# A seven-product cross network: layer 0 multiplies by C + 1, and its product 3 is split into seven smaller products

## The chip, the cores and the metric

The kernel runs on one core of a Trainium2 chip. The metric is the device time of one execution in microseconds (us). A time is the median of several executions; the profile is of one further execution.

## The reference

A deep cross network of six layers. The batch has 16384 rows of 1024 features, in bf16.

```python
B, F, D, L = 16384, 100, 16, 6
Din = min(F * D, 1024)          # 1024
# x0 [B, Din], ws [L, Din, Din], bs [L, Din], all bf16
def reference(x0, ws, bs):
    x = x0
    L = ws.shape[0]
    for l in range(L):
        proj = jnp.einsum('bd,de->be', x, ws[l]) + bs[l]
        x = x0 * proj + x
    return x
```

In layer 0 the state x is x0 itself, so that layer's result is x0 * (proj + 1).

## The kernel before

**Tiling.** The batch is cut into 16 pairs of 1024 rows. Eight super-rounds s = 0..7 each take two pairs, A and B, through the six layers, and each layer of one pair is a *step*: A layer 0, B layer 0, A layer 1 and so on, 96 steps in all. The state is kept transposed, features on the partitions: a `big` tile is [128, 2, 8, 512], where the second axis n says which 512 rows of the pair, the third which block of 128 features. A pair has one such tile for x0 (`x0T`) and one for its state (`xst`). The state tiles of A and of B are the same two buffers (big2, big3) in every super-round; those of x0 alternate.

**Seven products.** A step multiplies a 1024 x 1024 weight matrix with 1024 x 1024 data by one level of the Winograd form of Strassen's method: seven products of 512 x 512 instead of eight. A product is 16 matmuls of 128 x 128 weights and 512 data columns (`mm`, line 403), four for each 128 output features m. Product 1 goes to the four PSUM banks `pA`; products 6, 7 and 4 are added there one after the other. Product 5 goes to the four banks `pX`, and product 3 is added to it. ScalarE (ACT) copies each stage out of PSUM, with the bias where a stage begins a result (lines 52 and 55): P1s (product 1), P5s (product 5), S53 (5 + 3), U2s (1 + 6), C2[:, 1] (1 + 6 + 7), C2[:, 0] (1 + 6 + 7 + 4).

Product 2 (in every step but the first) and product 4 (after super-round 0) are split once more, each into seven products of 256 x 256. `inner` (line 411) is one such half-size product: four matmuls with 256 data columns. "Wide" and "narrow" matmuls below are those with 512 and 256 columns. The half-size products need combined weights (ids 8 for product 2 and 9 for product 4) and combined data (`ti2`, `ti4`, four parts of 512 columns each, made by `inner_t` as two differences t02, then t1, then t3). Their results are collected in EA and EB (product 2), and E4 and e5 (product 4).

**VectorE (DVE)** does all other arithmetic as two-operand operations recorded by `vtt` (line 46), in program order. For a step X, with Y the step before it (`prev`), it runs: T13 (the data of products 5 and 7, 4096 columns); then, of Y, m1 (C12 times x0), s11 (C22: C2[:, 1] + P5s), a1 (plus the state); X's T2 (product 6's data); Y's s4 (the parts of E4 that need e5); X's T4 (product 4's data); Y's e4 (C2[:, 0] + E4); the ti4 differences; Y's mC2 and aC2 (both halves of C2 times x0, plus the state, 4096 columns each), with t1 and t3 of ti4 before and behind aC2. Later come EA + EB, P1s + EA, the ti2 of the next step with m0 and a0 (C11 times x0, plus the state) between, and U2s + S53. T13, T2, T4, ti2 and ti4 have one buffer each.

```python
for f in (m1, s11, a1, t2, s4, t4, e4, i02, mC2, i1, aC2, i3):
```

**PSUM.** Eight banks in two pools of four, which change roles each step. In the pool `psX` stand first the three banks of product 2's half-size products, then the four of pX, then z5 and z1 of product 4's; each new bank waits for the copies out of the one that had the buffer.

**Order of the second half of a step.** Product 3 follows product 5 (its first column before product 5's last), then for product 6 one column and one half-size product of product 4 in turn, then product 7, then the rest of product 4; its last half-size product is deferred behind the next step's first column.

**Transfers.** SyncE (SP) issues all DMAs, in order. Weights sit in a ring of nine tiles shared by A and B; loads for the next layer are issued in B steps (`prefetch_upto`, line 99) and wait for PE to free a ring tile. In super-round 0 VectorE makes the combined weights (`combo`) and SP stores them to `Lc` in DRAM (line 139), from where later super-rounds load them. When a pair has ended, `turn_pair` (line 321) transposes its state tile by DMA into its old x0 tile, in the following step, once aC2 has written the last part; `write_pair` (line 328) then stores it. So A's state tile of super-round s - 1 is read by the transpose issued in B's layer 5, and B's by the one issued in A's layer 0 of super-round s.

`evt("P2s")` is a [128, 4, 512] buffer that holds product 2 in the first step alone.

Of the kernel before, what the change touches and what calls it, by code (L numbers as in the profile page):

```python
# [17 lines left out]
def kernel(  # L18
# [7 lines left out]
    nc = tc.nc  # L26
# [49 lines left out]
    def bank(p):  # L76
        return p.tile([P, NB], FP32, name="px")

    Lc = dram.tile([L, 6, P, KH * H], BF16, name="Lc")
    CIDX = {5: 0, 6: 1, 7: 2, 3: 3, 8: 4, 9: 5}  # L80
    lc = lambda l, pid: Lc[l, CIDX[pid]].rearrange("p (k e) -> p k e", k=KH)

    def raw_src(l, pid):
# [38 lines left out]
    def combo(l, pid):  # L122
        if pid <= 7:
            a, op, b = {5: (lambda: raw12[l], ADD, lambda: W[0, l, 4]), 6: (lambda: W[0, l, 5], SUB, lambda: W[0, l, 1]),
                        3: (lambda: W[0, l, 2], SUB, lambda: W[0, l, 6]), 7: (lambda: W[0, l, 1], SUB, lambda: raw12[l])}[pid]
            if pid == 5:
                W[0, l, 5] = ei_pool.tile([P, KH, H], BF16, name=("eb", "e4")[l % 2])
            t = W[0, l, pid]
            vtt(t[:], a()[:], b()[:], op)
        else:  # L130
            w = W[0, l, {8: 2, 9: 4}[pid]]
            t = W[0, l, 8] if pid == 8 else ti_pool.tile([P, KH, H], BF16, name="ti4")
            i11, i12, i21, i22 = w[:, 0:2, 0:HE], w[:, 0:2, HE:H], w[:, 2:4, 0:HE], w[:, 2:4, HE:H]
            iv = t[:].rearrange("p k (j e) -> p k j e", e=HE)
            vtt(iv[:, 0], i12, i22, ADD)
            vtt(iv[:, 3], i11, i12, SUB)
            vtt(iv[:, 1], iv[:, 0], i11, SUB)
            vtt(iv[:, 2], i21, iv[:, 1], SUB)
        pin(nc.sync.dma_start(lc(l, pid), t[:]))
# [1 line left out]
    def sub4(t):  # L141
        return {(i, j): t[:, 2 * i:2 * i + 2, j * NQ:(j + 1) * NQ] for i in range(2) for j in range(2)}

    def inner_t(hold, src, name):

        def t02():
            ti = ti_pool.tile([P, 4, 2, NQ], BF16, name=name)
            setattr(hold, name, ti)
            b = sub4(src())
            vtt(ti[:, 0], b[0, 1], b[0, 0], SUB)  # L150
            vtt(ti[:, 2], b[1, 1], b[0, 1], SUB)

        def t1():
            ti = getattr(hold, name)
            vtt(ti[:, 1], sub4(src())[1, 1], ti[:, 0], SUB)

        def t3():
            ti = getattr(hold, name)
            vtt(ti[:, 3], sub4(src())[1, 0], ti[:, 1], SUB)

        return [t02, t1, t3]
# [42 lines left out]
    ones = const.tile([P, P], BF16, name="ones")  # L204
    signs = const.tile([P, P], BF16, name="signs")
    nc.vector.memset(ones[:], 0.0)
    nc.vector.memset(ones[0:1, :], 1.0)
    nc.vector.memset(signs[:], 0.0)
    nc.vector.memset(signs[0:2, :], 1.0)
    nc.vector.memset(signs[0:1, :], -1.0)  # L210
# [38 lines left out]
    vcopy(b_all[:], pb[:, 0:LK])  # L249

    cur = {"A": Pair(0, x0T_A), "B": Pair(1, x0T_B)}
    new = {}
# [8 lines left out]
    def trail(Y, store):  # L261

        if Y is None:
            return [None] * 7
        C2, E4, e5 = Y.C2, Y.E4, Y.e5
        eh1 = lambda t: t[:, :, KH:KD, :]
        m1, a1 = fin_of(Y, Y.C12, 0, 1)

        def s4():
            for i in range(2):  # L270
                vtt(E4[:, 2 * i:2 * i + 2, NQ:NB], E4[:, 2 * i:2 * i + 2, (1 - i) * NQ:(2 - i) * NQ], e5[:], ADD)

        def a1s():
            a1()
            if store:
                store_half(Y, 0)

        return [m1, lambda: vtt(C2[:, 1], C2[:, 1], Y.P5s[:], ADD), a1s,
                s4 if E4 is not None else None,
                (lambda: vtt(C2[:, 0], C2[:, 0], E4[:], ADD)) if E4 is not None else None,  # L280
                lambda: vtt(C2[:], C2[:], eh1(Y.x0T), MULT),
                lambda: vtt(eh1(Y.xst), C2[:], eh1(Y.src_in), ADD)]

    def fin_of(Y, C, eh, n):
        xs = half(eh)
        return [lambda: vtt(C, C, Y.x0T[:, n, xs, :], MULT),
                lambda: vtt(Y.xst[:, n, xs, :], C, Y.src_in[:, n, xs, :], ADD)]

# [42 lines left out]
    for s in range(NPAIR // 2):  # L331
        for l in range(L):
            for side in ("A", "B"):
                X, Y = cur[side], prev
                first, last = step == 0, (X.pr, l) == LAST
                in2, in4 = not first, s > 0 and not (s + 1 == NPAIR // 2 and l + 1 == L)
                psA, psX = ps[step % 2], ps[1 - step % 2]
                step += 1
                bias = lambda eh, m, l=l: b_all[:, l * KD + eh * KH + m: l * KD + eh * KH + m + 1]
# [5 lines left out]
                def bring(who, s=s, home=home):  # L345
                    pr = 2 * (s + 1) + (who == "B")
                    new[who] = Pair(pr, bigt(home["n" + who]))
                    load_x0(pr, new[who].x0T)

                if side == "A" and s + 1 < NPAIR // 2:  # L350
                    if l == (2 if s > 0 else L - 1):
                        pending.append(lambda: bring("A"))
                    if l == 3 and s > 0:
                        pending.append(lambda: bring("B"))

                if s + 1 == NPAIR // 2 and side == "A" and l == 2:
# [8 lines left out]
                    pending.append(load_rows)  # L365

                def end_of(Y, late):
                    if s + 1 == NPAIR // 2 and side == "A" and l == L - 1 and not late:
# [19 lines left out]
                def mm(pid, wt, pts, m, start):  # L388
                    rhs = X.rhs(pid)
                    if last:  # L390
                        pt = pts[m][:]
                        if pid == 1:
                            nc.tensor.matmul(pt, lhsT=ones[:], rhs=zero[:], start=True, stop=False)  # L393
                        elif pid == 7:
                            nc.tensor.matmul(pt, lhsT=signs[:], rhs=zero[:], start=False, stop=False, skip_group_check=True)  # L395
# [42 lines left out]
                ev(P1s, pA, 0, 0)  # L438
                t2, t4 = (None, None) if first else (X.T2, X.T4)
                i02, i1, i3 = inner_t(X, lambda: X.T[4], "ti4") if in4 else [None] * 3  # L440
                for f in (m1, s11, a1, t2, s4, t4, e4, i02, mC2, i1, aC2, i3):
                    if f is not None:
                        f()
                if in2:
# [36 lines left out]
                    mm(5, w5, pX, 1, True)  # L481
                    inner(cols(q1), wi[:, 3], ti[:, 2], False)
                    evi(ea[1, 1], q1)
                    mm(5, w5, pX, 2, True)
                    inner(cols(q1), wr[1, 1], ti[:, 3], False)
                    evi(ea[1, 0], q1)
                    ev(P5s, pX, 1)
                    ev(P5s, pX, 2)
                    end_of(Y, False)
                    w3 = weights(3)  # L490
                    mm(3, w3, pX, 0, False)
                    mm(5, w5, pX, 3, True)
                    ev(P5s, pX, 3)
                    ev(S53, pX, 0, 0)
                    if not last:
                        ev(P1s, pA, 3, 0)
                    for m in range(1, KH):
                        mm(3, w3, pX, m, False)
                        ev(S53, pX, m, 0)
# [59 lines left out]
                if s == 0:  # L559
# [9 lines left out]
                    elif l + 1 < L:  # L569
                        for pid in (5, 6, 3) if l == 0 else ():  # L570
                            combo(1, pid)
                        combo(l + 1, 7)
                        combo(l + 1, 8)
                w6 = weights(6)
                end_of(Y, True)
                if last:
# [4 lines left out]
                X.C2, X.P5s, X.l = C2, P5s, l  # L581
                if in4:
                    w4, w4i, w7 = weights(4), weights(9), weights(7)
                    wj, wr4 = w4i[:].rearrange("p k (j e) -> p k j e", e=HE), sub_w(w4, HE)
# [3 lines left out]
                    e4 = sub4(E4)  # L588
                    z5, z1 = bank(psX), bank(psX)
                    mm(6, w6, pA, 0, False)  # L590
                    ev(U2s, pA, 0)
                    inner(cols(z1), wr4[0, 0], b4[0, 0], True)
# [4 lines left out]
                    evi(X.e5[:], z5)  # L597
                    mm(6, w6, pA, 2, False)
                    ev(U2s, pA, 2)
                    inner(cols(z1), wj[:, 1], t4[:, 1], False)  # L600
                    evi(e4[0, 1], z1)
                    mm(6, w6, pA, 3, False)
                    ev(U2s, pA, 3)
                    mm(7, w7, pA, 0, False)
                    ev(C2[:, 1], pA, 0, 1)
                    inner(cols(z1), wj[:, 3], t4[:, 2], False)
                    evi(e4[1, 0], z1)
                    for m in range(1, KH):
                        mm(7, w7, pA, m, False)
                        ev(C2[:, 1], pA, m, 1)  # L610
                    col = lambda m0, j, pA=pA: (lambda m: pA[m0 + m][:, j * NQ:(j + 1) * NQ])
                    inner(col(0, 0), wr4[1, 0], b4[1, 0], False)
                    inner(col(0, 1), wj[:, 2], b4[1, 1], False)
# [79 lines left out]
```

## Time and profile before

| | |
|---|---|
| median of 3 runs | 2267.81 us (2267.52 to 2268.53) |
| the profiled execution, its own time | 2268.03 us |
| its span | 2266.2 us, 33559 instructions |
| busy share of the span | PE 100%, weight loads 56%, DVE 95%, ACT 84% |
| DMA | 334.59 MB, mean 148 GB/s |

Each line of a timeline has the start in us from the span's start, the busy time, the engine, the line of the kernel, the operation with output and inputs, the count of merged instructions, and in brackets the idle time before and what ended it. PE is TensorE's matmul, PEld its weight load, SPq the DMA queue of SP. Matmuls overlap, so their rate is read from starts.

### The profile page before, as it was taken

The page shows a single profiled execution, that of the slowest core. Times are in us where ns is not written, and L with a number is a line of the kernel's source. Part 1 is how long each engine was busy: PE and PEld are TensorE (multiplying, and loading weights), DVE is VectorE, ACT ScalarE, POOL GpSimd, SP SyncE. Part 2 cuts the span into 40 slices and gives each one's busy share as a digit, 9 for nine tenths or more (in the row PEclk, how much of TensorE's full clock was granted, in tenths as well). Part 3 has the DMA queues.
Part 4 walks back from the last instruction along what each step waited for, and adds up shares of the span by engine and source line. Part 5 has one row for each costly group of instructions (what it writes and reads, how often), then busy time and mean ns, then how long its engine had stood idle before and what let it go on. Part 6 is the DMA issues. An engine that isn't in the chain of part 4 may idle for free.

```text
span 2266.2 us, 33559 instructions
## 1 busy us (share of the span) xinstructions
PE 2259.2 (100%) x12925; PEld 1264.4 (56%) x12925; DVE 2161.6 (95%) x2394; ACT 1910.9 (84%) x3307; POOL 0.7 (0%) x6
## 2 busy tenths in 40 slices
PE   9999999999999999999999999999999999999999
PEld 4555555555555555555555555555555555555554
DVE  8999989999999999999999999999999999999999
ACT  6777788888888888888888888888888888888887
POOL 0000000000000000000000000000000000000000
PEclk9999999999999999999999999999999999999999
DMA  7423494523945239442494434944348443483337
GB/s 231 151 94 121 149 216 159 146 85 119 255 133 136 93 124 257 132 121 97 128 259 122 121 112 127 245 121 121 125 124 236 121 131 121 126 228 121 104 119 178
DMA packets 508452, 334.59 MB, mean 148 GB/s; under 512 B 390530, under 2 KB 470404, under 8 KB 508292
## 3 DMA queue, kind: packets, MB, share of 16 engines
q1 hardware_dynamic: 508292, 332.45, 51.7%
q8 instruction: 101, 1.65, 0.3%
q14 instruction: 59, 0.48, 0.1%
HBM read 213.92 MB, written 52.43 MB: 118 GB/s over the span
## 4 chain that ended last, share of the span: by engine, by line
PE 99%; DMA 0%; DVE 0%; SPq 0%; issue 0%; ACT 0%; DVEq 0%
PE px L403 74%; PE px L411 24%; PE px L398 1%; DMA wp<-in_ws_dram 0%; DVE cb L46 0%; SPq L120 0%; DVE eb L46 0%; DVE T L46 0%; DVE wp L46 0%; SPq L217 0%; PE px L395 0%; PE px L393 0%; ACT cb L52 0%; SPq L220 0%; DVEq L46 0%
## 5 line engine op out<-in xcount | busy, mean ns | idle before, releaser
L403 PEld LDWEIGHTS <-wp 128*128 128x128 bf16 x7344 | 718.5, 98 | 669.9 <-issue 0.8
L403 PE MATMUL px<-T,wp 128*128 128x512 bf16 x4384 | 1069.4, 379 | 0.0
L403 PE MATMUL px<-big,wp 128*128 128x512 bf16 x2960 | 712.4, 379 | 0.4 <-ACT big L52 0.4
L411 PEld LDWEIGHTS <-wp 128*128 128x128 bf16 x4752 | 465.0, 98 | 254.3
L55 ACT ACTIVATE cb<-px,b_all 128x512 bf16<-128x512 f32 x760 | 502.0, 686 | 85.3 <-PE px L403 71.4
L411 PE MATMUL px<-ti,wp 128*128 128x256 bf16 x2684 | 402.7, 273 | 0.0
L52 ACT CAST ea<-px 128x512 bf16<-128x512 f32 x344 | 201.6, 586 | 140.5 <-PE px L411 140.5
L46 DVE TENSOR_TENSOR T<-big 128x4096 bf16<-128x4096 bf16 (+1 forms) x97 | 220.1, 2269 | 71.0 <-PE px L403 71.0
L52 ACT CAST U2s<-px 128x512 bf16<-128x512 f32 x384 | 225.0, 586 | 64.4 <-PE px L403 61.4
L55 ACT ACTIVATE P1s<-px,b_all 128x512 bf16<-128x512 f32 x380 | 254.3, 695 | 6.0 <-PE px L403 4.4
L55 ACT ACTIVATE S<-px,b_all 128x512 bf16<-128x512 f32 x380 | 242.3, 703 | 0.8 <-PE px L403 0.8
L46 DVE TENSOR_TENSOR T<-big,T 128x2048 bf16<-128x2048 bf16 x192 | 234.1, 1219 | 1.4
L52 ACT CAST P5s<-px 128x512 bf16<-128x512 f32 x384 | 217.9, 596 | 17.7 <-PE px L403 17.5
L46 DVE TENSOR_TENSOR cb<-cb,big 128x4096 bf16<-128x4096 bf16 (+2 forms) x105 | 221.6, 2113 | 0.7 <-ACT cb L52 0.5
L46 DVE TENSOR_TENSOR big<-cb,big 128x4096 bf16<-128x4096 bf16 x95 | 217.2, 2286 | 0.5
L52 ACT CAST e<-px 128x512 bf16<-128x512 f32 x328 | 192.7, 588 | 0.0
L411 PE MATMUL px<-big,wp 128*128 128x256 bf16 x1084 | 162.6, 273 | 0.0
L52 ACT CAST eb<-px 128x512 bf16<-128x512 f32 x258 | 152.1, 590 | 6.2
L411 PE MATMUL px<-T,wp 128*128 128x256 bf16 x984 | 134.2, 273 | 0.0
L46 DVE TENSOR_TENSOR P1s<-P1s,big 128x2048 bf16<-128x2048 bf16 x106 | 129.3, 1220 | 3.3 <-ACT P1s L55 2.4
L46 DVE TENSOR_TENSOR S<-U2s,S 128x2048 bf16<-128x2048 bf16 (+1 forms) x97 | 117.2, 1208 | 2.5 <-ACT U2s L52 2.4
L46 DVE TENSOR_TENSOR S<-S,big 128x2048 bf16<-128x2048 bf16 (+1 forms) x99 | 118.5, 1197 | 0.1
(77 smaller groups left out, 1360.8 us busy)
## 6 DMA issues: line engine op xcount, KB each, us to landing
wp<-Lc SPq DMA_DIRECT2D x252, 512.0 KB, 4.6
wp<-in_ws_dram SPq DMA_DIRECT2D x144, 512.0 KB, 3.4
out_dram<-big SPq DMA_DIRECT2D x28, 1024.0 KB, 10.7
Lc<-big SPq DMA_DIRECT2D x15, 512.0 KB, 2.7
Lc<-wp SPq DMA_DIRECT2D x9, 512.0 KB, 2.7
ea<-in_ws_dram SPq DMA_DIRECT2D x6, 512.0 KB, 5.2
Lc<-ti SPq DMA_DIRECT2D x6, 512.0 KB, 3.1
big<-in_x_dram SPq DMA_DIRECT2D x1, 2048.0 KB, 9.9
```

Source lines behind the costliest of these rows:

```text
L46: return pin(nc.vector.tensor_tensor(out=out, in0=in0, in1=in1, op=op))
L52: return pin(nc.scalar.copy(out=out, in_=in_))
L55: return pin(nc.scalar.activation(out=out, in_=in_, func=IDENT, bias=bias, scale=1.0))
L398: nc.tensor.matmul(pt, lhsT=rhs[:, k, m * P:(m + 1) * P], rhs=wt[:, k, :], start=(start and k == 0 and pid != 1), stop=(k == KH - 1), **kw)
L403: nc.tensor.matmul(pts[m][:], lhsT=wt[:, k, m * P:(m + 1) * P], rhs=rhs[:, k, :], start=(start and k == 0), stop=(k == KH - 1), **kw)
L411: nc.tensor.matmul(dst(m), lhsT=w[:, k, m * P:(m + 1) * P], rhs=rhs[:, k, :], start=(start and m == 0 and k == 0), stop=(k == 1), skip_gro ...
```

## The change

In layer 0 the state added at the end is x0 itself. The change adds 1 to the biases of layer 0 when they are set up, multiplies by x0 straight into the state tile, and leaves out a1, a0 and aC2 there (the name aC2 is then that of nothing; mC2 writes the state). This holds in all 16 steps of layer 0.

In the 14 steps of layer 0 after super-round 0 (`in3`), product 3 is done by seven half-size products. Its combined weights have id 10; they are made in super-round 0 and loaded once per super-round into the buffer of P2s. Its combined data `ti3` (made by k02, k1, k3) lies in the second half of the pair's new state tile; the collected E3 lies in another quarter of it; e6 is a new small buffer. Three of the seven half-size products are added in pX, four go to two further banks y1 and y5. In the next step m1 completes E3 with e6, adds it to C12, and multiplies. The order of VectorE's work with ti3 differs between A and B. The two constant tiles `ones` and `signs` of the last step are set later, by GpSimd, in the ti4 buffer.

```diff
+    Lc = dram.tile([L, 7, P, KH * H], BF16, name="Lc")
...
+    pin(nc.vector.tensor_scalar_add(out=b_all[:, 0:KD], in0=pb[:, 0:KD], scalar1=1.0))
+    vcopy(b_all[:, KD:LK], pb[:, KD:LK])
...
+        if Y.E3 is not None:
+            def m1(E3=Y.E3, e6=Y.e6, C=Y.C12, mul=m1):
+                for i in range(2):
+                    vtt(E3[:, 2 * i:2 * i + 2, NQ:NB], E3[:, 2 * i:2 * i + 2, (1 - i) * NQ:(2 - i) * NQ], e6[:], ADD)
+                vtt(C, C, E3, ADD)
+                mul()
...
-                lambda: vtt(C2[:], C2[:], eh1(Y.x0T), MULT),
-                lambda: vtt(eh1(Y.xst), C2[:], eh1(Y.src_in), ADD)]
+                lambda: vtt(eh1(Y.xst) if Y.l == 0 else C2[:], C2[:], eh1(Y.x0T), MULT),
+                None if Y.l == 0 else (lambda: vtt(eh1(Y.xst), C2[:], eh1(Y.src_in), ADD))]
...
+        if Y.l == 0:
+            return [lambda: vtt(Y.xst[:, n, xs, :], C, Y.x0T[:, n, xs, :], MULT), None]
...
+                X.l, in3 = l, l == 0 and s > 0
...
+                if side == "B" and s + 1 < NPAIR // 2 and l == L - 1:
+                    w3i = evt("P2s")
+                    pending.insert(0, lambda w=w3i: pin(nc.sync.dma_start(w[:], lc(0, 10))))
...
-                for f in (m1, s11, a1, t2, s4, t4, e4, i02, mC2, i1, aC2, i3):
+                if in3:
+                    ti3 = X.xst[:, 0, KH:KD, :].rearrange("p q (k b) -> p q k b", k=2)
+                    k02, k1, k3 = inner_t(X, lambda: X.rhs(3), "ti3", ti3)
+                order = (m1, s11, a1, t2, k02, s4, k1, t4, k3, e4, i02, mC2, i1, aC2, i3)
+                if in3 and side == "B":
+                    order = (m1, s11, a1, t2, s4, t4, e4, k02, i02, k1, k3, mC2, i1, aC2, i3)
+                for f in order:
...
+                    if in3:
+                        ev(P5s, pX, 1)
                     mm(5, w5, pX, 2, True)
                     inner(cols(q1), wr[1, 1], ti[:, 3], False)
                     evi(ea[1, 0], q1)
...
+                        inner(colx(0, 0), wr3[1, 0], b3[1, 0], False)
+                        inner(colx(0, 1), wk[:, 2], b3[1, 1], False)
+                        ev(S53, pX, 0, 0)
+                        mm(5, w5, pX, 3, True)
+                        ev(P5s, pX, 3)
+                        ev(S53, pX, 1, 0)
+                        ev(P1s, pA, 3, 0)
...
                     mm(6, w6, pA, 0, False)
+                    if in3:
+                        inner(colx(2, 0), wr3[1, 1], t3[:, 3], False)
+                        ev(S53, pX, 2, 0)
+                        ev(S53, pX, 3, 0)
                     ev(U2s, pA, 0)
+                    if in3:
+                        y1, y5 = bank(psX), bank(psX)
+                        X.E3 = X.xst[:, 1, 0:KH, :]
...
+                    if in3:
+                        inner(cols(y1), wr3[0, 0], b3[0, 0], True)
+                        evi(e3[0, 0], y1)
...
```

The lines left out place the other three half-size products of y1 and y5 with their copies behind columns of products 6 and 7, make and store the combined weights, and set the two constant tiles.

More of the change, by code (lines that the diff above doesn't have):

```diff
@@ L77, in bank @@
         return p.tile([P, NB], FP32, name="px")
-    Lc = dram.tile([L, 6, P, KH * H], BF16, name="Lc")
-    CIDX = {5: 0, 6: 1, 7: 2, 3: 3, 8: 4, 9: 5}
+    Lc = dram.tile([L, 7, P, KH * H], BF16, name="Lc")
+    CIDX = {5: 0, 6: 1, 7: 2, 3: 3, 8: 4, 9: 5, 10: 6}
     lc = lambda l, pid: Lc[l, CIDX[pid]].rearrange("p (k e) -> p k e", k=KH)
@@ L130, in combo @@
         else:
-            w = W[0, l, {8: 2, 9: 4}[pid]]
+            w = W[0, l, {8: 2, 9: 4, 10: 3}[pid]]
             t = W[0, l, 8] if pid == 8 else ti_pool.tile([P, KH, H], BF16, name="ti4")
@@ L142, in sub4, with inner_t @@
         return {(i, j): t[:, 2 * i:2 * i + 2, j * NQ:(j + 1) * NQ] for i in range(2) for j in range(2)}
-    def inner_t(hold, src, name):
+    def inner_t(hold, src, name, tile=None):
         def t02():
-            ti = ti_pool.tile([P, 4, 2, NQ], BF16, name=name)
+            ti = tile if tile is not None else ti_pool.tile([P, 4, 2, NQ], BF16, name=name)
             setattr(hold, name, ti)
@@ L203 @@
     b_all = const.tile([P, LK], FP32, name="b_all")
[L204 to L210, printed above, removed]
     home = dict(xA=0, xB=1, sA=2, sB=3, nA=4, nB=5)
@@ L273, in a1s @@
         def a1s():
-            a1()
+            if a1 is not None:
+                a1()
             if store:
@@ L365 @@
                     pending.append(load_rows)
+                if s + 1 == NPAIR // 2 and side == "A" and l == L - 1:
+                    rowsel = ti_pool.tile([P, 4, 2, NQ], BF16, name="ti4")
+                    ones, signs = rowsel[:, 0, 0, 0:P], rowsel[:, 1, 0, 0:P]
+                    nc.gpsimd.memset(rowsel[:, 0:2, 0, 0:P], 0.0)
+                    nc.gpsimd.memset(ones[0:1, :], 1.0)
+                    nc.gpsimd.memset(signs[0:2, :], 1.0)
+                    nc.gpsimd.memset(signs[0:1, :], -1.0)
                 def end_of(Y, late):
@@ L392, in mm @@
                         if pid == 1:
-                            nc.tensor.matmul(pt, lhsT=ones[:], rhs=zero[:], start=True, stop=False)
+                            nc.tensor.matmul(pt, lhsT=ones, rhs=zero[:], start=True, stop=False)
                         elif pid == 7:
-                            nc.tensor.matmul(pt, lhsT=signs[:], rhs=zero[:], start=False, stop=False, skip_group_check=True)
+                            nc.tensor.matmul(pt, lhsT=signs, rhs=zero[:], start=False, stop=False, skip_group_check=True)
                         for k in range(KH):
@@ L440 @@
                 i02, i1, i3 = inner_t(X, lambda: X.T[4], "ti4") if in4 else [None] * 3
-                for f in (m1, s11, a1, t2, s4, t4, e4, i02, mC2, i1, aC2, i3):
+                X.E3 = None
+                k02, k1, k3 = [None] * 3
+                if in3:
[5 more added lines that the diff above has]
+                for f in order:
                     if f is not None:
@@ L486 @@
                     evi(ea[1, 0], q1)
-                    ev(P5s, pX, 1)
+                    if not in3:
+                        ev(P5s, pX, 1)
                     ev(P5s, pX, 2)
@@ L490 @@
                     w3 = weights(3)
[L491 to L495, printed above, removed]
-                        ev(P1s, pA, 3, 0)
-                    for m in range(1, KH):
-                        mm(3, w3, pX, m, False)
-                        ev(S53, pX, m, 0)
+                    if in3:
+                        wk, wr3 = w3i[:].rearrange("p k (j e) -> p k j e", e=HE), sub_w(w3, HE)
+                        b3, t3 = sub4(X.rhs(3)), X.ti3
+                        colx = lambda m0, j, pX=pX: (lambda m: pX[m0 + m][:, j * NQ:(j + 1) * NQ])
+                        inner(colx(0, 0), wr3[1, 0], b3[1, 0], False)
[4 more added lines that the diff above has]
+                        ev(S53, pX, 1, 0)
+                        ev(P1s, pA, 3, 0)
+                    else:
+                        mm(3, w3, pX, 0, False)
+                        mm(5, w5, pX, 3, True)
+                        ev(P5s, pX, 3)
+                        ev(S53, pX, 0, 0)
+                        if not last:
+                            ev(P1s, pA, 3, 0)
+                        for m in range(1, KH):
+                            mm(3, w3, pX, m, False)
+                            ev(S53, pX, m, 0)
                     vtt(e0(EA), e0(EA), e0(EB), ADD)
@@ L573 @@
                         combo(l + 1, 8)
+                        if l == 0:
+                            combo(0, 10)
                 w6 = weights(6)
@@ L580 @@
                 C2 = cb_pool.tile([P, 2, KH, NB], BF16, name="cb")
-                X.C2, X.P5s, X.l = C2, P5s, l
+                X.C2, X.P5s = C2, P5s
                 if in4:
@@ L590 @@
                     mm(6, w6, pA, 0, False)
+                    if in3:
+                        inner(colx(2, 0), wr3[1, 1], t3[:, 3], False)
+                        ev(S53, pX, 2, 0)
+                        ev(S53, pX, 3, 0)
                     ev(U2s, pA, 0)
+                    if in3:
+                        y1, y5 = bank(psX), bank(psX)
+                        X.E3 = X.xst[:, 1, 0:KH, :]
+                        X.e6 = ei_pool.tile([P, 2, NQ], BF16, name="e6")
+                        e3 = sub4(X.E3)
                     inner(cols(z1), wr4[0, 0], b4[0, 0], True)
@@ L597 @@
                     evi(X.e5[:], z5)
+                    if in3:
+                        inner(cols(y1), wr3[0, 0], b3[0, 0], True)
+                        evi(e3[0, 0], y1)
                     mm(6, w6, pA, 2, False)
@@ L601 @@
                     evi(e4[0, 1], z1)
+                    if in3:
+                        inner(cols(y5), wk[:, 0], t3[:, 0], True)
+                        evi(X.e6[:], y5)
                     mm(6, w6, pA, 3, False)
                     ev(U2s, pA, 3)
+                    if in3:
+                        inner(cols(y1), wk[:, 1], t3[:, 1], False)
+                        evi(e3[0, 1], y1)
                     mm(7, w7, pA, 0, False)
@@ L610 @@
                         ev(C2[:, 1], pA, m, 1)
+                        if in3 and m == 1:
+                            inner(cols(y1), wk[:, 3], t3[:, 2], False)
+                            evi(e3[1, 0], y1)
                     col = lambda m0, j, pA=pA: (lambda m: pA[m0 + m][:, j * NQ:(j + 1) * NQ])
```

1 line of the change is left out of this document (removed).

## The prediction

> **What bounds the kernel now.** I read the page first: busy times, the chain that ended last, the group that shows where VectorE (DVE) waits.
>
> ```profile
> PE 2259.2 (100%) x12925; PEld 1264.4 (56%) x12925; DVE 2161.6 (95%) x2394; ACT 1910.9 (84%) x3307; POOL 0.7 (0%) x6
> ...
> PE 99%; DMA 0%; DVE 0%; SPq 0%; issue 0%; ACT 0%; DVEq 0%
> ...
> L46 DVE TENSOR_TENSOR T<-big 128x4096 bf16<-128x4096 bf16 (+1 forms) x97 | 220.1, 2269 | 71.0 <-PE px L403 71.0
> ```
>
> TensorE (PE) is the chain; DVE idles 71 us, always for PE. A busy PE could still stall inside the modelled ends, so next the timeline of PE: two step starts of super-round 0, then the A step of layer 0 in super-round 2 (it runs from 575.10 to 598.48).
>
> ```profile
> 80.99 2.75 PE L403 MATMUL px<-big,wp 128*128 128x512 bf16 x12
> ...
> 104.76 2.75 PE L403 MATMUL px<-big,wp 128*128 128x512 bf16 x12
> ...
> 586.36 2.75 PE L403 MATMUL px<-big,wp 128*128 128x512 bf16 x12
> 588.95 1.03 PE L403 MATMUL px<-T,wp 128*128 128x512 bf16 x4
> ...
> 597.61 1.04 PE L411 MATMUL px<-T,wp 128*128 128x256 bf16 x8
> 598.48 1.03 PE L403 MATMUL px<-big,wp 128*128 128x512 bf16 x4
> ```
>
> Twelve wide matmuls start 2.59 us before the next block, 0.2158 each; eight narrow ones 0.87, 0.109 each. A step of 80 wide and 56 narrow lasts 23.38, so a narrow one is (23.38 - 17.27)/56 = 0.1092. Super-round 0 has 96 wide and 28 narrow: 20.72 + 3.06 = 23.78, and its two step starts are 23.77 apart. So no step has a stall, and the time of a step is its matmuls.
>
> Then DVE in that A step, from its wait for PE to the next:
>
> ```profile
> 574.43 2.29 DVE L46 TENSOR_TENSOR T<-big 128x4096 bf16<-128x4096 bf16 x1 [0.84 <-PE px L403]
> 576.63 1.22 DVE L46 TENSOR_TENSOR S<-S,big 128x2048 bf16<-128x2048 bf16 x1
> 577.77 1.22 DVE L46 TENSOR_TENSOR cb<-cb,P5s 128x2048 bf16<-128x2048 bf16 x1
> ...
> 587.32 2.29 DVE L46 TENSOR_TENSOR big<-cb,big 128x4096 bf16<-128x4096 bf16 x1
> ...
> 595.74 1.22 DVE L46 TENSOR_TENSOR S<-U2s,S 128x2048 bf16<-128x2048 bf16 x1
> 597.81 2.29 DVE L46 TENSOR_TENSOR T<-big 128x4096 bf16<-128x4096 bf16 x1 [0.85 <-PE px L403]
> ```
>
> Only 0.85 us of a step is free on DVE. Starts are 2.21 apart after 4096 columns, 1.135 after 2048, 0.335 after 512.
>
> ScalarE (ACT) evicts at 0.48 to 0.49 per copy; SyncE (SP) issues the transposes of ended pairs:
>
> ```profile
> 583.53 0.59 ACT L52 CAST ea<-px 128x512 bf16<-128x512 f32 x1 [0.17 <-PE px L411]
> 584.84 0.59 ACT L52 CAST ea<-px 128x512 bf16<-128x512 f32 x1 [0.71 <-PE px L411]
> 585.32 1.08 ACT L52 CAST P5s<-px 128x512 bf16<-128x512 f32 x2
> ```
>
> ```profile
> 566.26 10.46 SPq L321 DMA_TRANSPOSE big<-big  x1
> ...
> 589.64 12.55 SPq L321 DMA_TRANSPOSE big<-big  x1
> ```
>
> **The change part by part.** Times below count from a step's first matmul of product 1.
>
> Product 3, in the 14 steps of layer 0 after super-round 0: out go 16 wide matmuls (3.453 us), in come 28 narrow ones (3.057). The instruction lists agree: 224 wide fewer, 392 narrow more. Without stalls such a step takes 22.98: 14 x 0.397 = 5.55 us less. More can't come from these steps, since before has no stall in them to remove.
>
> That halving the width halves the time rests on rows of this kernel: 56 narrow matmuls per step at 0.109 with a weight load of 98 ns beside each. [...] The rows, 216 and 109, decide.
>
> VectorE loses three additions per step of layer 0: 1.135 + 1.135 + 2.21 = 4.48, in 16 steps. It gains, in 14 steps, four differences (ti3, 1.34), two additions of e6 (0.67) and C12 + E3 (1.135): 3.15. That is lighter overall; what counts is order and first use.
>
> A step: the difference tile begins behind T2. T13 -0.67, m1 1.54, s11 2.67, a1 3.81, T2 4.94, first two differences 6.08, e4 additions 6.75, k1 7.42, T4 7.76, k3 8.89, ended 9.31. PE wants k3 at the half-product after product 6's first column: 9 x 0.8633 + 10 x 0.4367 = 12.14. The last DVE operation, U2s + S53, starts near 20.98, so the next T13 could start at 22.11; PE releases it at 22.98 - 0.67 = 22.31. Nothing stalls, but only 0.2 is spare.
>
> B step: here the previous step's E3 comes first, and it is a chain. Two dependent operations cost extra: in the timeline of DVE near 308, one of 1.23 from 307.79 is followed by its dependent at 309.05, 0.04 after its end. So: e6 additions 1.54 and 1.87, C12 + E3 2.33, its product with x0 3.59, s11 4.73, T2 5.86, e4 7.00, T4 7.67, e4 sum 8.80, differences 9.94, those of ti4 10.61, k1 11.28, k3 11.74, ended 12.16. PE starts 0.06 after a DVE result (at the kernel's start T ends at 16.10, its matmul starts at 16.16), at 12.22 instead of 12.14. So PE stalls about 0.08 in each of 7 B steps: 0.55 us. Below, the bound is zero; above, if the three dependent links and k3's wait cost like the longest hand-over in this view (0.11, behind the two ea additions), 0.08 + 4 x 0.07 = 0.36 each, 2.5 in all. I take 0.08, since single waits are what the list shows.
>
> ACT: four more copies per changed step (e3 three times, e6), 4 x 0.49 = 1.9, beside 20.1 busy of 23.4. P5s column 1 moves ahead of the last ea copy: 583.53 is 8.43, so it starts at 8.92 and ends 9.51; the half-product that overwrites its bank wants it at 9.54 + 0.22. The ea copy stays at 9.74 and ends 10.33; product 5's last column takes that bank at 10.41, as now. Then S53 0 at 10.71, P5s 3 at 11.48, S53 1 at 11.97, P1s 12.56, S53 2 at 13.13, ended 13.82; its bank is wanted by y1 at 14.31. The queue runs up to 1.5 late and has caught up by product 7's third column, at 21.45. Taken at zero; with every hand-over 0.1 late, 14 x 0.1 = 1.4.
>
> The transposes: ti3 and E3 lie in the pair's new state tile, which the ended pair's transpose still reads. In the A step differences start at 6.08. That transpose is issued at 566.26 (14.54 in the step before) and asked one by one those of A land 12.3 to 14.1 after issue: at most 14.54 + 14.1 - 23.38 = 5.26. In the B step the order writes them at 9.94. The issue at 589.64 (14.54) waits for the end of aC2, which ti3 moves from 14.51 to 15.85; the B ones took 13.3 to 15.5, so 8.40 at most, but in super-round 1, where SP issues it only at 309.57 behind the loads and it takes 17.0: 326.6, which is 9.1. Zero, with 0.1 for that one. Should a landing be late, ti3 waits at the head of DVE's queue and with it T4, ti4, mC2 and k3, which PE needs.
>
> The added loads (one product-3 tile per super-round, L99's neighbours on SP) are issued early in layer 5's B step, at a time when the loads behind them still wait for PE to free a ring tile; 512 KB from Lc took 4.6 to land (the page's DMA issues), and first use is 9.5 into the next step. Hidden; if it pushed the transpose, that is the rival below. Weights of product 4 are wanted 2 us earlier (12.6); issued at 577.43 (2.33), they would land at 8.6 even at the 6.3 us that such loads take between 590 and 620. The combination for these weights adds 1.34 of DVE in super-round 0, less than the additions gone there. Memsets on GpSimd run a step before use; the bias addition sits in a 3.6 us idle of DVE. All zero.
>
> Sum: -5.55 + 0.55 + 0.1 = -4.9. On the profiled execution, 2268.03, that is 2263.1; on the median, 0.22 lower, 2262.9.
>
> **Rivals.**
> *Longer chain in B* (0.27): the hand-overs cost towards their upper bound, with ACT's 0.1. For: DVE reaches k3 within 0.1 of its use, so every delay is PE's. Against: in all steps of before such chains fit. Between 1 and 4.5 lost: 2263.4 to 2266.5, about 2264.5; no difference to be told.
> *Late transpose* (0.11), slower: k02 in the B step waits for the ended pair's transpose, PE behind it. It decides once landing passes 9.94 in B; each us later costs 7. With more DMA traffic ahead (asked for 590 to 620, the hardware queue is busy 100.4%, with two output writes of 1 MB among its issues), a landing at 12 gives 7 x (12 - 9.94 + 0.08) = 15: 2277.3. Against: landings 1.5 us early.
> *DVE is the bound* (0.03): at 95% its work falls 16 x 4.48 - 14 x 3.15 - 1.3 = 26 us, giving 2241.6. Against: its idle is for PE in each step. [...]
> *Weight loads show* (0.02): if the 98 ns stood bare behind narrow matmuls, 392 x 0.098 = 38 us: 2267.8 - 5.55 + 38.4 = 2300.7. Against: the start-to-start 0.109.
> That nothing changes in the work is excluded by the counts.
>
> **How the numbers follow.** A measurement here can tell about 0.2%, 4.5 us, from no change: faster means below 2263.3. The forecast (0.57) with 2262.2 to 2263.3, and DVE as bound, make 0.60 faster; the longer chain 0.27 the same; late transposes and weight loads 0.13 slower. The range joins the first two cases, with a little below for a chain that costs nothing: 2261.8 to 2266.5.
>
> **What would show it.** Right: steps of 22.98 (A) and 23.06 (B) between step starts, with 28 narrow matmuls more, and a PE wait for DVE on big of under 0.1 in B. Wrong: A steps above 23.1 (ACT, banks); B steps above 23.3 with DVE waiting for nothing (chain) or for DMA (transpose); PE waiting for DMA on weights.

## The result, and the profile after

The changed kernel takes 2263.57 us (median of 18 runs, 2262.65 to 2265.75) against 2267.86 for the kernel before on the same chip (18 runs, 2267.51 to 2270.63). The ratio is 0.9981 with a 95% interval of 0.9974 to 0.9988: 4.3 us or 0.19% less. The interval does not contain 1, so the change is clear of noise; but its middle lies just inside the 0.2% that the prediction took as the bound of "faster". The profiled execution, one of the 18, took 2263.38, span 2261.6 (before: 2268.03 and 2266.2).

From the page of the kernel after: the busy line, the chain by engine, the weight loads of the narrow matmuls with the idle time in front of them, and the group in which VectorE (DVE) waits.

```profile
PE 2253.6 (100%) x13093; PEld 1279.8 (57%) x13093; DVE 2140.2 (95%) x2444; ACT 1930.2 (85%) x3363; POOL 1.6 (0%) x10
...
PE 99%; DMA 0%; DVE 0%; SPq 0%; issue 0%; ACT 0%; DVEq 0%
...
L427 PEld LDWEIGHTS <-wp 128*128 128x128 bf16 x4920 | 480.8, 98 | 257.4 <-DVE big L46 2.8
...
L46 DVE TENSOR_TENSOR T<-big 128x4096 bf16<-128x4096 bf16 (+1 forms) x97 | 220.1, 2269 | 77.9 <-PE px L419 77.2
```

TensorE (PE) is still the chain, and DVE's largest wait is still for PE. The one new thing stands in the third line: weight loads of narrow matmuls wait 2.8 us for a DVE result on big. The list of waits gives it as 7 waits of 0.4 each, one per B step of layer 0 after super-round 0. In this trace a weight load starts one matmul ahead of its own (the one for the wide matmul of 609.63 at 609.42), so little of that 0.4 reaches the matmuls. How much is read from PE's timeline of the kernel after, here at the A and the B step of layer 0 in super-round 2:

```profile
574.73 1.03 PE L419 MATMUL px<-big,wp 128*128 128x512 bf16 x4
...
596.84 1.04 PE L427 MATMUL px<-T,wp 128*128 128x256 bf16 x8
597.71 1.03 PE L419 MATMUL px<-big,wp 128*128 128x512 bf16 x4
...
608.12 1.89 PE L419 MATMUL px<-T,wp 128*128 128x512 bf16 x8
609.92 0.61 PE L427 MATMUL px<-big,wp 128*128 128x256 bf16 x4
...
620.78 1.03 PE L419 MATMUL px<-big,wp 128*128 128x512 bf16 x4
```

The A step lasts 597.71 - 574.73 = 22.98, the B step 620.78 - 597.71 = 23.07. Eight narrow matmuls take 0.87, as before. The eight wide ones from 608.12 need 8 x 0.2158 = 1.73, so the narrow ones on big should start at 609.85; they start at 609.92, 0.07 late. The rest of the 0.09 is lost within these four matmuls.

The same B step in DVE's timeline of the kernel after:

```profile
595.70 1.22 DVE L46 TENSOR_TENSOR S<-U2s,S 128x2048 bf16<-128x2048 bf16 x1
597.04 2.29 DVE L46 TENSOR_TENSOR T<-big 128x4096 bf16<-128x4096 bf16 x1
...
606.51 1.22 DVE L46 TENSOR_TENSOR cb<-cb,e 128x2048 bf16<-128x2048 bf16 x1
607.65 0.75 DVE L46 TENSOR_TENSOR big<-big 128x512 bf16<-128x512 bf16 x2
...
608.99 0.87 DVE L46 TENSOR_TENSOR big<-big,big 128x512 bf16<-128x512 bf16 x2
...
620.11 2.29 DVE L46 TENSOR_TENSOR T<-big 128x4096 bf16<-128x4096 bf16 x1 [1.24 <-PE px L419]
```

T13 starts 0.67 before the step, e4's sum at 606.51, then come the first differences of ti3 and ti4, and k1 and k3 (started at 608.99) end at 609.86. PE starts on them 0.06 later. The last line shows 1.24 us of idle time in the B step, where before had 0.85; in the A step only 597.04 - (595.70 + 1.135) = 0.2 is left.

Sum over the steps: fourteen lose 0.397, seven give 0.09 back: -4.9. The spans differ by 4.6. The missing 0.3 lies ahead of everything the change was priced for: PE's first wait for a data tile in super-round 0, in the timelines of before and then of after.

```profile
16.16 3.63 PE L403 MATMUL px<-T,eb 128*128 128x512 bf16 x16 [0.83 <-DVE T L46]
```

```profile
16.49 3.63 PE L419 MATMUL px<-T,eb 128*128 128x512 bf16 x16 [1.73 <-DVE T L46]
```

The line in the kernel after starts 0.33 later. DVE was late there because its first addition waited 1.14 us for a weight load, and in the profile of before 0.25; both began at the landing, at 12.81 and 12.48.

### The profile page after: what moved, and what is told of

Read it like the earlier page. It is cut to its first block, busy times and chain, and to the rows that moved or that the text cites. A ratio compares the mean times of both kernels' runs of the same rounds, so it can differ in the third digit from the quotient of the medians.

```text
span 2261.6 us, 33979 instructions
## 1 busy us (share of the span) xinstructions
PE 2253.6 (100%) x13093; PEld 1279.8 (57%) x13093; DVE 2140.2 (95%) x2444; ACT 1930.2 (85%) x3363; POOL 1.6 (0%) x10
## 4 chain that ended last, share of the span: by engine, by line
PE 99%; DMA 0%; DVE 0%; SPq 0%; issue 0%; ACT 0%; DVEq 0%
PE px L419 72%; PE px L427 26%; PE px L414 1%; DMA wp<-in_ws_dram 0%; DVE cb L46 0%; SPq L120 0%; DVE eb L46 0%; DVE T L46 0%; SPq L210 0%; PE px L411 0%; PE px L409 0%; DVE wp L46 0%; ACT cb L52 0%; SPq L213 0%; DVEq L46 0%
## 5 line engine op out<-in xcount | busy, mean ns | idle before, releaser
L419 PE MATMUL px<-big,wp 128*128 128x512 bf16 x2736 | 659.3, 379 | 0.4 <-ACT big L52 0.4
L52 ACT CAST e<-px 128x512 bf16<-128x512 f32 x342 | 204.4, 606 | 0.0
L427 PE MATMUL px<-big,wp 128*128 128x256 bf16 x1252 | 187.9, 273 | 0.0
L46 DVE TENSOR_TENSOR cb<-cb,big 128x4096 bf16<-128x4096 bf16 (+2 forms) x89 | 184.9, 2080 | 0.7 <-ACT cb L52 0.5
L46 DVE TENSOR_TENSOR cb<-cb,P5s 128x2048 bf16<-128x2048 bf16 (+1 forms) x97 | 117.1, 1208 | 0.1
L46 DVE TENSOR_TENSOR P1s<-P1s,big 128x2048 bf16<-128x2048 bf16 x90 | 109.7, 1219 | 7.9 <-ACT P1s L55 7.8
```

The costliest lines, as they stand in the source:

```text
L46: return pin(nc.vector.tensor_tensor(out=out, in0=in0, in1=in1, op=op))
L52: return pin(nc.scalar.copy(out=out, in_=in_))
L419: nc.tensor.matmul(pts[m][:], lhsT=wt[:, k, m * P:(m + 1) * P], rhs=rhs[:, k, :], start=(start and k == 0), stop=(k == KH - 1), **kw)
L427: nc.tensor.matmul(dst(m), lhsT=w[:, k, m * P:(m + 1) * P], rhs=rhs[:, k, :], start=(start and m == 0 and k == 0), stop=(k == 1), skip_gro ...
```

## The experiments

The theory: the gain is the shorter sum of matmuls in the 14 steps, less a stall of under 0.1 in each B step where DVE reaches k3 a little late; DVE's saved work brings nothing by itself, but makes room for the split. Rivals: DVE's relief is the gain; a longer chain; the late transpose; and, for the missing 0.3 to 0.6, a first step that the change makes longer. Diffs are against the changed kernel. A step time is that between the first copies of product 1 in successive steps; the first step's, taken so up to the second step's copy, is 26.64 in the profile of before. "A steps 22.98" below is meant of super-rounds 2 to 7: in super-round 1 the A step's first copy is not held up by a deferred half-size product, and this measure gives 24.27 before and 23.87 with the split, again 0.40 less.

**k1 and k3 ahead of e4 in B.** One operation, C2[:, 0] + E4, goes behind ti3's last part.

```diff
-  order = (m1, s11, a1, t2, s4, t4, e4, k02, i02, k1, k3, mC2, i1, aC2, i3)
+  order = (m1, s11, a1, t2, s4, t4, k02, i02, k1, k3, e4, mC2, i1, aC2, i3)
```

> Undoes one thing: in the B step the chain k02, i02, k1, k3 stands before the e4 sum instead of behind it, so k3 ends near 11.0 instead of 12.16. Theory (matmul sum plus one 0.09 us wait of PE for k3 in each B step): B steps fall from 23.07 to 22.98, PE has no wait for DVE there, 7 x 0.09 = 0.6 us less than the changed kernel, about 2263.0. Rival (the excess over 22.98 in B is a bank or an ACT hand-over, not k3): B steps stay at 23.07 and the time stays. Rival (transposes): differences now want the state tile 1.1 us earlier, at 8.80; transposes landed at 5.4 to 7.1 into the B step, 9.3 in super-round 1; so at most that one step waits on DVE, 0.5 us, which PE does not see.

Measured: 2262.29 (9 runs, 2261.95 to 2264.05), ratio to before 0.9975 (0.9965 to 0.9984). All seven B steps last 22.98. In PE's timeline of this kernel the narrow matmuls now follow the eight wide ones without a gap:

```profile
607.74 1.89 PE L419 MATMUL px<-T,wp 128*128 128x512 bf16 x8
609.47 0.60 PE L427 MATMUL px<-big,wp 128*128 128x256 bf16 x4
```

607.74 to 609.47 is 1.73, eight wide matmuls and nothing else. So the 0.09 per B step was k3's lateness and only that. In super-round 1 DVE waits 0.46 for the transpose, as expected, and PE does not see it. The medians of this kernel and the changed one differ by more than 0.6, but the two ratios' intervals overlap; the steps carry this verdict, not the medians.

**The biases alone.** C + 1 stays, product 3 is whole again, without its weights and their loads.

```diff
-                X.l, in3 = l, l == 0 and s > 0
+                X.l, in3 = l, False
...
-                if side == "B" and s + 1 < NPAIR // 2 and l == L - 1:
-                    w3i = evt("P2s")
-                    pending.insert(0, lambda w=w3i: pin(nc.sync.dma_start(w[:], lc(0, 10))))
...
-                        if l == 0:
-                            combo(0, 10)
```

> One part alone: C + 1 in layer 0 (its state additions gone, 4.48 us of VectorE per step), but product 3 with 16 wide matmuls everywhere, and no weights 10. Theory (PE is the bound): all steps after super-round 0 stay at 23.38, the time equals the kernel before within 0.5 us, DVE is idle about 4.5 us more in each of 16 steps. Rival (DVE at 95% is the bound): 16 x 4.48 = 72 us less, 2196.

Measured: 2268.15 (10 runs), ratio 1.0001 (0.9992 to 1.001). Its page, the busy line and DVE's wait:

```profile
PE 2259.7 (100%) x12925; PEld 1261.6 (56%) x12925; DVE 2093.3 (92%) x2342; ACT 1909.6 (84%) x3307; POOL 1.6 (0%) x10
...
L46 DVE TENSOR_TENSOR T<-big 128x4096 bf16<-128x4096 bf16 (+1 forms) x97 | 220.2, 2270 | 95.6 <-PE px L416 95.6
```

DVE is busy for 68 us less than before, waits for PE 25 us longer in this group, and every step lasts what it did (23.38 in layer 0 from the second super-round on). The rival that DVE is the bound has fallen.

**The split alone.** The biases are without the 1, and the three additions of the state are back.

```diff
-    pin(nc.vector.tensor_scalar_add(out=b_all[:, 0:KD], in0=pb[:, 0:KD], scalar1=1.0))
-    vcopy(b_all[:, KD:LK], pb[:, KD:LK])
+    vcopy(b_all[:], pb[:, 0:LK])
...
-                lambda: vtt(eh1(Y.xst) if Y.l == 0 else C2[:], C2[:], eh1(Y.x0T), MULT),
-                None if Y.l == 0 else (lambda: vtt(eh1(Y.xst), C2[:], eh1(Y.src_in), ADD))]
+                lambda: vtt(C2[:], C2[:], eh1(Y.x0T), MULT),
+                lambda: vtt(eh1(Y.xst), C2[:], eh1(Y.src_in), ADD)]
...
-        if Y.l == 0:
-            return [lambda: vtt(Y.xst[:, n, xs, :], C, Y.x0T[:, n, xs, :], MULT), None]
```

> The other part alone: product 3 in seven half-size products as in the changed kernel, but biases without 1 and the three state additions of layer 0 kept. Theory (PE sum plus DVE's chain): A steps 22.98; A's a0 makes the next T13 late by about 0.8, B's a1 adds 1.14 before k3, so k3 ends near 14.1 and PE waits about 2.0 us in each B step: B steps near 25.0, time 2263.6 + 7 x 1.9 = 2277, slower than before. Rival (C + 1 is not needed for the split, DVE has room): as the changed kernel, 2263.6.

Measured: 2276.2 (4 runs, 2275.21 to 2277.07), ratio 1.0035 (1.0022 to 1.0049): slower than before. A steps 22.98; B steps 24.88 in five, 24.08 in super-round 1, 26.91 in super-round 3 (the last section tells why). From its list of waits (time in all, count, longest):

```profile
PE px L424 <- DVE big L46: 11.7, 7, 2.1
```

The narrow matmuls cost the same here as in the changed kernel (four in 0.43), but in B PE waits for k3: 1.7 us of idle time in five steps, 0.9 in super-round 1 and 2.1 in super-round 3. The steps of the five are 1.90 over their matmuls, near the 2.0 expected. So the two halves of the change need each other: C + 1 gives nothing alone, and the split alone, with this order of DVE's work, loses 8 us. The split alone with k1 and k3 ahead of e4 was not run.

**One order for A and B.** B writes ti3 as early as A.

```diff
-                if in3 and side == "B":
-                    order = (m1, s11, a1, t2, s4, t4, e4, k02, i02, k1, k3, mC2, i1, aC2, i3)
```

> B takes A's order: differences right behind T2, wanted at 7.0 of the B step, where the transpose of the ended pair landed at 5.4 to 7.1 in the changed kernel (9.3 in super-round 1). Theory: where it has landed, k3 ends near 10.2 and B steps are 22.98; in super-round 1 DVE waits 2.3 us and PE about 1; in all 0 to 1.5 us beside the changed kernel, 2263 to 2264.5. Rival (transposes decide, as in the slower case of the prediction): DVE waits for DMA in most B steps, B steps above 23.3, over 2266.

Measured: 2264.25 (10 runs, 2262.98 to 2265.68), ratio 0.9982 (0.9973 to 0.9991). Six B steps last 22.98, that of super-round 1 25.51. DVE's timeline of this kernel in that step, which starts at 317.46 (T13 + 0.67):

```profile
323.33 1.22 DVE L46 TENSOR_TENSOR T<-big,T 128x2048 bf16<-128x2048 bf16 x1
327.95 0.76 DVE L46 TENSOR_TENSOR big<-big 128x512 bf16<-128x512 bf16 x2 [3.41 <-DMA big<-big]
```

This is the mechanism of the late transpose: the first difference of ti3 waits at the head of DVE's queue for the DMA that still reads the state tile, until 10.5 into the step. DVE loses 3.41 (2.3 was expected) and PE 2.5 behind it (about 1 was expected), in two waits: 1.5 for ti3, and then 0.7 for ti4, which the same queue had held up. It happens only in super-round 1. In the changed kernel the transpose is issued there at 310.67, 3.90 behind the end of aC2 (0.06 in super-round 2), since two loads of x0 and two stores stand ahead of it on SP, and it takes 16.5 to land; five of the other six land 12.6 to 14.2 after their issue, 5.4 to 7.1 into the step, and the trace has no landing for the sixth. In this profiled execution the single order thus trades seven stalls of 0.09 for one of 2.5. The median, 0.7 above the changed kernel's, is less than the difference of 1.9 that the steps give, but within the scatter of both; whether each execution has the stall at this size is not shown.

**One operation too many in B, or in A.** An extra DVE operation of 2048 columns ahead of k02; it writes the place of ti3, and nobody uses its result.

```diff
+  dum = lambda: vtt(X.xst[:, 0, KH:KD, :], X.x0T[:, 1, KH:KD, :], X.x0T[:, 0, KH:KD, :], SUB)
-  order = (m1, s11, a1, t2, s4, t4, e4, k02, i02, k1, k3, mC2, i1, aC2, i3)
+  order = (m1, s11, a1, t2, s4, t4, e4, dum, k02, i02, k1, k3, mC2, i1, aC2, i3)
```

> The changed kernel with one more 2048-column VectorE operation (1.135 us, a difference that is overwritten) ahead of k02 in the B steps. Theory: k3 has no slack, so PE's wait grows by just that: B steps 23.07 + 1.13 = 24.20, in all 8 us more, about 2271.5. Rival (there is slack that the chain of starts does not show, or PE waits for something else there): B steps 23.07 to 23.5.

Measured (one run): 2271.55, before 2268.25 beside it. B steps 24.10, in super-round 1 24.97; A steps 22.98. So PE pays 24.10 - 23.07 = 1.03 in the step and nothing in the next, since the B step has 1.24 of idle time at its end. That the 1.03 is near 1.135 is in part chance. On DVE the operation costs 1.26: from the start of the part that writes ti3's place to the next difference, of ti4, it is 611.58 - 609.65 = 1.93, against 608.32 - 607.65 = 0.67 in the changed kernel. The extra 0.12 fits a dependent start (0.04 behind the end instead of 0.08 ahead of it), since k02 writes over the result. PE's timeline of this kernel in the B step that starts at 599.71:

```profile
611.84 0.38 PE L427 MATMUL px<-T,wp 128*128 128x256 bf16 x2
613.18 0.60 PE L427 MATMUL px<-big,wp 128*128 128x256 bf16 x4 [0.95 <-DVE big L46]
```

The matmuls on ti3 start 13.47 into the step, against 12.21 in the changed kernel: 1.26 later, all that DVE lost. But two matmuls of the next half-size product, which stood behind them, stand ahead of them in this kernel's instructions, and fill 0.22 of the wait: 1.26 - 0.22 = 1.04. In super-round 1 the extra operation itself waits 0.79 for the transpose, which lands 10.8 into the step there.

```diff
+  dumA = (lambda: vtt(X.xst[:, 0, KH:KD, :], X.x0T[:, 1, KH:KD, :], X.x0T[:, 0, KH:KD, :], SUB)) if in3 and side == "A" else None
-  order = (m1, s11, a1, t2, k02, s4, k1, t4, k3, e4, i02, mC2, i1, aC2, i3)
+  order = (m1, s11, a1, t2, dumA, k02, s4, k1, t4, k3, e4, i02, mC2, i1, aC2, i3)
```

> The same extra operation ahead of k02 in the A steps. Theory: k3 of A was 2.8 us early, so A steps stay at 22.98; but only 0.2 of DVE's time was spare, so the next T13 is 0.93 late and with it the whole chain of B: B steps 23.07 + 0.93 = 24.0, about 2270. Rival (a step's delay stays in the step): A and B as in the changed kernel, 22.98 and 23.07.

Measured (one run): 2270.12. A steps 22.98, yet the B steps behind them 24.12, but for super-round 1 (23.07), where DVE has idle time in the A step that takes the delay. PE's and DVE's timelines of this kernel in the B step of super-round 2, which starts at 598.14:

```profile
611.40 0.61 PE L427 MATMUL px<-big,wp 128*128 128x256 bf16 x4 [0.96 <-ACT P1s L55]
```

```profile
610.47 0.88 DVE L46 TENSOR_TENSOR big<-big,big 128x512 bf16<-128x512 bf16 x2
```

The operation stands in A and the stall in B: with only 0.2 to spare at the end of the A step, 1.05 of the 1.26 that the operation costs here, too, is handed over (T13 starts 0.38 behind the step's start instead of 0.67 ahead of it), and the B step is 24.12 - 23.07 = 1.05 longer. The releaser named is a copy of ScalarE (ACT) that ended at 611.36, 13.2 into the step. In the changed kernel it ends 13.2 into the step as well, where these matmuls start at 12.2, ahead of its end; so they do not wait for it. What does end at 611.35 is k3 on DVE: the name of a wait can be a neighbour of its cause.

**The changed kernel once more**, with nothing altered, for the first step.

> The changed kernel once more, on the chip and beside the runs of the next one. Theory: 14 steps give 14 x 0.397 - 7 x 0.09 = 4.9 us less than before; what a median lies off that is the first step, where PE waits for the first combined weights (0.8 to 2.5 us in the profiles so far, and once at half clock for 3.4 us): steps 22.98 and 23.07 again, first step between 26.6 and 30. Rival (the change made the first step slower): first step above 27 in each profile of it.

Measured: 2263.36 (11 runs, 2262.56 to 2264.62), before 2268.25 (20 runs), ratio 0.9979 (0.997 to 0.9988). Its steps are those of the first profile, but the first lasts 26.72 instead of 27.54, PE's first data wait is 0.9, and the span is 2261.3, just 4.9 below that of before. So the late first step is not in each run of the change. In this comparison the medians, too, differ by 4.9.

**The order of the first experiment, with the extra weights loaded once.**

```diff
-                if side == "B" and s + 1 < NPAIR // 2 and l == L - 1:
+                if side == "B" and s == 0 and l == L - 1:
...
```

> The early chain of k02, i02, k1, k3 in B, and the weights of product 3 loaded once into the buffer of P2s rather than once per super-round. Theory: the loads were hidden, so as with the early chain alone: A and B 22.98, 5.5 us under before, 2262.6, 0.6 under the changed kernel. Rival (the loads delayed the transposes or the ring): more than 1 us under the early chain alone, or transposes landing over 0.5 us earlier in layer 0.

Measured: 2262.75 (10 runs, 2261.84 to 2265.33), ratio 0.9977 (0.9967 to 0.9986). A and B steps 22.98, as with seven loads: the loads were hidden, and leaving out six brings nothing. The transposes land 0.4 us earlier in the B steps of layer 0 than in the first experiment (the mean of the five super-rounds that both traces have), less than the rival asked for, and no step is shorter for it. The order of the first experiment (0.9975 there, 0.9977 here) is the best version found, by its steps 0.6 us below the changed kernel.

## Why the prediction was right

The cause was as told, and the terms came out one by one. The time alone does not show it: 2263.57 lies above the 2262.2 to 2263.3 that the prediction gave its own forecast, just inside the 2263.4 to 2266.5 of its longer chain in B. It is the steps that tell the two apart. The B steps are 0.09 over their matmuls, against 0.08 forecast and up to 0.36 for the longer chain; the 0.7 by which the first median lies above the forecast is not in them.

- Product 3 by narrow matmuls: 22.98 forecast and measured in the A steps. The 0.109 for a narrow matmul, read from before, holds in the changed kernel with a weight load of 98 ns beside each: 0.87 for eight.
- The chain in B: 23.06 forecast, 23.07 measured; k3 forecast to end 12.16 into the step, measured 609.86 - 597.71 = 12.15. The three dependent links at 0.04 each were the right choice between the ends given; the upper end (0.36 per step) did not come. The first experiment shows the term to be k3's alone.
- The spare time in A: 0.2 forecast and measured, and the delay put into A shows that it is no more.
- ACT's four copies per step, the loads and GpSimd's memsets: nothing, as taken. In the A step of super-round 2 the copies from P5s column 1 to S53 2 start within 0.03 of the times forecast (the first at 583.65, 8.92 into the step). No A step is longer than its matmuls, and one load in place of seven changes nothing. The memsets were not tried apart.
- The transposes: at most 8.40 into the B step forecast, and 9.1 in super-round 1; 5.4 to 7.1 and 9.3 measured. So the first bound held and that of super-round 1 was 0.2 too low. In the two profiles of the changed kernel no landing is late, but in super-round 1 this is partly luck: in five more profiles, of kernels that are the same up to that B step, it came 8.7 to 10.8 into the step (8.7 in the changed kernel once more, 10.8 with one operation more in B), and ti3 is wanted at 9.94. The rival's mechanism is real there, as the single order shows, with a landing at 10.5.
- The 0.1 kept for super-round 1 was not needed in these two profiles; by the landings at 10.5 and 10.8 some executions may need more.
- DVE as the bound and bare weight loads fell: the former by the biases alone, the latter by the A step.
- One reading of the profile before was too wide: the 71.0 us are the idle time of one group. In all DVE is idle for 2266.2 - 2161.6 = 104.6 us, and some of its waits are for ScalarE (6.2 us ahead of P1s). Nothing in the sum hangs on it.

The forecast was 2262.9. The first comparison gave 0.7 more, the second 0.5 more, beside a kernel before that was 0.4 slower than in the first. The term the forecast held fixed is the first step: in the profiles here it lasts between 26.64 and 28.61 (30.03 with the halved clock of the last section), as PE's first data wait lasts 0.8 to 2.8. Whether the change makes that wait longer on the average can only be told from the medians, since most timed runs leave no profile. The biases alone, whose other steps are those of before, have nearly the median of before (2268.15 against 2268.21). For the whole change the medians give 4.3 and 4.9 where the steps give 4.9; for the order of the first experiment 5.9 and, with one load, 5.5, where the steps give 5.6. So no lasting lengthening is seen; the 0.6 that the first comparison lacks is within its interval, and no run tells its cause.

## What to carry to other kernels

When the slowest engine has no stall, the worth of an edit is its change in that engine's instruction sum, and the work saved on another engine is worth only the room it makes; here 68 us less of VectorE's work gave nothing by itself, and without that room the split lost 8 us. Give each operation a due time counted from the step's start and compare it with the due time of its user: here a chain that was 0.08 late by this count showed as a stall of 0.09 in each B step, and moving one operation that was not yet waited for behind it took the stall away. Look for idle time at the end of the step, too: where it was 0.2, a delay of 1.26 reappeared in the next step as 1.05, under another engine's name.

## What the runs showed of the hardware that was not expected

After a PE wait, of 2.09 us in one kernel and of 2.54 in another, the clock was granted at half for 3.41 us. In the split-only kernel the B step of super-round 3 lasted 26.91 instead of 24.88. Its PE timeline, from the wait on:

```profile
892.29 0.27 PE L424 MATMUL px<-T,wp 128*128 128x256 bf16 x1
894.65 0.93 PE L424 MATMUL px<-big,wp 128*128 128x256 bf16 x4 [2.09 <-DVE big L46]
...
896.02 1.91 PE L416 MATMUL px<-T,wp 128*128 128x512 bf16 x4
897.73 0.83 PE L424 MATMUL px<-ti,wp 128*128 128x256 bf16 x4
898.39 0.60 PE L424 MATMUL px<-big,wp 128*128 128x256 bf16 x4
```

Four wide matmuls take 897.73 - 896.02 = 1.71 instead of 0.86, and from 898.39 on the pace is normal. The records of the clock put it at half for 3.41 us, from 894.77 to 898.18, which is 1.7 lost; the wait itself was 2.09 instead of 1.74, and the two make up the 2.03.

```profile
891.36:894.77 3.41, 1.32 (x9) 0.59 (x7) 3.38 (x8) 1.94 (x4) 0.00 (x0) 1.00 0.90 213
894.77:898.18 3.41, 3.41 (x14) 1.81 (x13) 3.41 (x3) 2.44 (x5) 0.00 (x0) 0.50 0.81 186
```

These are the stretch with the wait and the one behind it. The second figure of a line is its length, the third PE's busy time; the last three columns are the granted clock, the DMA share and GB/s.

The profiled execution of the kernel with the biases alone had the same behind its first wait, of 2.54 us, again for 3.41 us, from 17.70 to 21.11. Its clock over the five microseconds around that:

```profile
17.00:22.00 5.00, 4.64 (x14) 1.82 (x15) 5.00 (x6) 1.32 (x3) 0.00 (x0) 0.66 1.26 238
```

Half clock for 3.41 of 5.00 gives just this 0.66. The 16 wide matmuls behind the wait take 22.51 - 17.36 = 5.15, against 19.62 - 16.16 = 3.46 in the profile of before; the first step lasts 30.03, the time is 2270.89 against a median of 2268.15.

It is no matter of the wait's length alone. The wait of 2.80 at the start of the kernel with one load was not followed by half clock: its first step, 28.61, is longer than the 26.64 of before by 1.97, just as its wait is (2.80 against 0.83). Nor were the six other waits of the split alone, 0.9 and five times 1.7. What else decides is not shown: with two cases of half clock, these profiles give no rule for it.
